# Linear attention and a gated layer on one core: the queues of all engines through the attention written out in steps

## The chip, the cores and the metric

The kernel runs on one core of a Trainium2 chip. The metric is device time in microseconds (us). The core has a matrix engine (TensorE, PE in the profile), a vector engine (VectorE, DVE), a scalar engine (ScalarE, ACT), GpSimd (POOL) and an engine that issues transfers (SyncE, SP). Each works through a queue of its own, and semaphores hold an instruction until what it needs is there.

## What is computed

First comes linear attention over 8 batches of 8 heads, 576 positions and 64 dimensions, with 128 features. Its output, 4608 rows of 512, then goes through a gated layer with 1536 hidden units.

```python
def phi(x):
    proj = np.einsum('bhsd,df->bhsf', x, w_phi)
    proj = proj - np.max(np.abs(proj), axis=-1, keepdims=True)
    return np.concatenate([np.exp(proj), np.exp(-proj)], axis=-1)
q_p, k_p = (phi(q), phi(k))
kv = np.einsum('bhsf,bhsd->bhfd', k_p, v)
z = np.sum(k_p, axis=2)
num = np.einsum('bhsf,bhfd->bhsd', q_p, kv)
den = np.einsum('bhsf,bhf->bhs', q_p, z)[..., None] + 1e-06
...
gate = 1.0 / (1.0 + np.exp(-(x @ w_gate)))
val = x @ w_val
return (gate * val @ w_out).astype(np.float32)
```

## The kernel before

**The steps of the attention.** Two heads are worked together, so there are 32 steps, four to a batch. A step i has these pieces:

- `q_half` (twice) and `k_heads`, `k_rest`: projections pq and pk on TensorE. ScalarE copies pq into d; VectorE takes the maximum mx of each row of pk, subtracts it (dk), and ScalarE takes the exponentials ek. For the first two steps (`DIRECT`) ScalarE reads pk itself.
- `q_max`: VectorE finds the maximum over the features of the queries (pm, pn), spreads it (mb) and subtracts it from d.
- `kv`: the products of keys and values (kvz), copied by ScalarE (kvt). `turn` transposes it (tp, then the copy kv).
- `q_exp`: ScalarE's exponentials eq of the queries, read from d.
- `num`: numerators nm and denominators dp, copied by ScalarE into ex and dr.
- `norm` and `scale`: the denominators go through three transfers, dn (out of dr), den (to memory, after VectorE's reciprocal) and rb (back, spread over the rows). VectorE then multiplies ex by rb (xp), and xp is stored to `xscr`.

From step 4 on GpSimd adds up ek (su) so that kvz needs fewer matmuls.

**The gated layer.** The 1536 hidden units are 12 groups of 128. The first five (`JA`) are worked in chunks of 256 rows between the pieces of the attention; the other seven follow in a second phase (`rest_chunks`), in chunks of 512 rows. Each product of a row and a weight is three matmuls of high and low parts (xh, xl, wh, wl). An item of the first phase is either a `half` (12 matmuls into gv, for the gate's or the value's 128 units) or a `half_out` (15 matmuls into acc, copied by ScalarE into y and stored). After the second half of a pair, `gated` makes the gated hidden units: t and u on ScalarE, three operations on VectorE, hh on ScalarE, hl on VectorE. The weights arrive as 64-bit floats and are split by `from_f64`, five VectorE operations and one ScalarE operation a tile; `TILES` says how many tiles are asked for by which step. gv has two buffers, acc one, and five PSUM banks rotate through all the attention's products.

**What sets the order.** TensorE's order is the program's. `fill` is called four times a step and puts in as many items as are due; items of a batch become due `LAG` calls after the batch's last step is queued. All other engines and the transfers are ordered by the tool's scheduler. It is steered by `attend`, which gives the attention a higher priority, and by `issue_after`, which ties weights behind the last subtraction of the queries (`marks`).

Of the kernel before, what the change touches and what calls it, by code (L numbers as in the profile page):

```python
# [37 lines left out]
PRIORITY = 400  # L38
RATE = 3.0
LAG = (5, 8)  # L40
TILES = (1, 2, 4, 7, 11, 15)
# [3 lines left out]
def attention_moe(  # L45
# [29 lines left out]
    def from_f64(h, l, raw, mid, sp, nb, name):  # L75
# [10 lines left out]
        if mid is None:  # L86
            rest, unit = hi, lo
            vec.tensor_scalar(
                hi, hi, 16, 0x01FF0000, op0=ALU.logical_shift_left, op1=ALU.bitwise_and
            )  # L90
            vec.scalar_tensor_tensor(
                hi, lo, 16, hi, op0=ALU.logical_shift_right, op1=ALU.bitwise_or
            )
        else:
            words = mid.rearrange("p (n two) -> p n two", two=2)
            rest, unit = words[:, :, 0], words[:, :, 1]
            vec.tensor_scalar(rest, rest, 0x01FFFFFF, None, op0=ALU.bitwise_and)
# [5 lines left out]
    def load_weights(j, m, wp, sp, nb, twice):  # L103
# [7 lines left out]
        load, mid = nc.sync.dma_start(raw, w_moe[j, :, m, :].bitcast(U32)), None  # L111
        if twice:

            mid = sp.tile([P, 2 * DM], U32, tag="wmid", name=f"wmid{j}_{m}", bufs=nb)
            nc.sync.dma_start(
                mid[:, : 2 * DM - 1].bitcast(U16),
                w_moe[j, :, m, :].bitcast(U16)[:, 1 : 4 * DM - 1],
            )
        return load, *from_f64(wh[:, ms], wl[:, ms], raw, mid, sp, nb, f"{j}_{m}")
# [41 lines left out]

    def half_units(js, mp, ps_gv, ps_acc):
        xs, hs, gvs, cs = {}, {}, {}, set()

        def begin(c, marks=()):
            if c in cs and c not in xs:
                xh, xl, raw = x_tiles(mp, CH, f"1_{c}")
                nc.sync.dma_start(raw, xscr[c])
                with ExitStack() as stack:
                    behind(stack, marks)  # L170
                    split(xh, xl, raw)
                xs[c] = xh, xl

        def half(c, i, m):
            begin(c)
# [5 lines left out]
            if m == 1:  # L181
                hs[c, i] = gated(gv[:, 0, :], gv[:, 1, :], CH, mp, 6, n)
                if i >= 1:
                    begin(c + 1, hs[c, i][2])

        def half_out(c, t):
            acc = ps_acc.tile([P, DM], F32, tag="acc", name=f"acc1_{c}_{t}")
            for i, j in enumerate(js):
                mm_out(acc, t, hs[c, i], j, i == 0, i == len(js) - 1)
            y = mp.tile([P, DM], F32, tag="y", name=f"y1_{c}_{t}", bufs=1)  # L190
# [3 lines left out]
        def chunk(c):  # L194
# [74 lines left out]
    with ExitStack() as actx:  # L269
        wp1 = actx.enter_context(tc.tile_pool(name="wp1", bufs=1))  # L270
# [19 lines left out]
        with tc.high_priority(offset=2 * PRIORITY):  # L290
            nc.sync.dma_start(wk, w_phi)
# [4 lines left out]
        loaded, ks, ds, kvs, marks, rbs = {}, {}, {}, {}, [], {}  # L296
# [10 lines left out]
        def load_kv(i):  # L307
            b, p = steps[i]
            n = f"{b}_{p}"
            kx = at.tile([P, 5 * P], F32, tag="kin", name="k" + n)  # L310
            nc.sync.dma_start(kx, k[b, p])
            vx = at.tile([P, 10, D], F32, tag="vin", name="v" + n)
            nc.sync.dma_start(vx, v[b, p])
            loaded["k", i], loaded["v", i] = kx, vx

        def q_half(i, hf):
# [11 lines left out]
            for hd in range(2):  # L328
                act.copy(d[:, hd, cs], pps[hd])

        def k_exp(i, g, pp, ns):
            n = f"{i}_{g}"
            mx = at.tile([P, 4], F32, tag="mx", name="mx" + n)
            vec.tensor_reduce(  # L334
                mx[:, :ns], pp[:, :ns, :], axis=AX.X, op=ALU.max,
                apply_absolute_value=True,
            )
            e = at.tile([P, ns, 2 * F], F32, tag=f"ek{ns}", name="ek" + n, bufs=6 - ns // 2)
            if i < DIRECT:
                mn = at.tile([P, 4], F32, tag="mn", name="mn" + n)  # L340
                vec.tensor_scalar(mn[:, :ns], mx[:, :ns], -1.0, None, op0=ALU.mult)
                for t in range(ns):
                    for sg in (1, 0):
                        act.activation(
                            e[:, t, sg * F : sg * F + F], pp[:, t, :], AF.Exp,
                            bias=(mn, mx)[sg][:, t : t + 1], scale=1.0 - 2.0 * sg,
                        )
            else:
                dk = at.tile([P, ns, F], F32, tag=f"dk{ns}", name="dk" + n)
                vec.tensor_tensor(  # L350
                    dk, pp[:, :ns, :],
                    mx[:, :ns].unsqueeze(2).broadcast_to([P, ns, F]),
                    op=ALU.subtract,
                )
                for sg in range(2):
                    act.activation(  # L356
                        e[:, :, sg * F : sg * F + F], dk, AF.Exp, scale=1.0 - 2.0 * sg
                    )
            ks.setdefault(i, []).append(e)

        def k_heads(i):
# [8 lines left out]
            for hd in range(2):  # L370
                k_exp(i, hd, pps[hd], 4)

        def k_rest(i):
            kx = loaded.pop(("k", i))
            pp = bank([P, 4, F], f"pk{i}_2")
            nc.tensor.matmul(pp[:, 0, :], kx[:, 4 * P :], wk, start=True, stop=True)
            k_exp(i, 2, pp, 1)
            if i < EARLY:
                return

# [12 lines left out]

        def q_max(i):
            d = ds[i]
# [8 lines left out]
            )  # L404
            vec.tensor_copy(pn[0:64], pm[64:128])
# [5 lines left out]
            vec.tensor_tensor(pm, pm, pn, op=ALU.max)  # L411
            vec.transpose(  # L412
# [3 lines left out]
            marks.append(vec.tensor_tensor(d, d, mb, op=ALU.subtract))  # L416

        def kv(i):
# [26 lines left out]
            kvt = at.tile([P, 3 * F], F32, tag="kvt", name=f"kvt{i}")  # L445
# [11 lines left out]
        def q_exp(i):  # L457
            d = ds.pop(i)
            es = []
            for sg in range(2):  # L460
                e = at.tile([P, 2, S], F32, tag=f"eq{sg}", name=f"eq{i}_{sg}")
                act.activation(e, d, AF.Exp, scale=1.0 - 2.0 * sg)
                es.append(e)
            ds[i] = es

        def num(i):
            es, w = ds.pop(i), kvs.pop(i)
# [22 lines left out]
            act.copy(dr, dp)  # L490
            for hf in range(2):
                act.copy(ex[:, hf * HS : hf * HS + HS], nms[hf])
            rbs[i] = (ex, dr)

        def norm(i):
            ex, dr = rbs[i]
            dn = at.tile([P, 9], F32, tag="dn", name=f"dn{i}")
            rb = at.tile([P, S], F32, tag="rb", name=f"rb{i}", bufs=1)
            nc.sync.dma_start(
                dn, dr.rearrange("(o r) c -> o r c", r=Q)[:, 0, :]  # L500
            )
            vec.tensor_scalar(dn, dn, 1e-6, None, op0=ALU.add)
            vec.reciprocal(dn, dn)
            nc.sync.dma_start(dens[i].rearrange("h (r c) -> (h r) c", c=9), dn)
            for hd in range(2):
# [3 lines left out]
            rbs[i] = (ex, rb)  # L509

        def scale(i):
            b, p = steps[i]
            ex, rb = rbs.pop(i)
            xp = at.tile([P, S], F32, tag="xp", name=f"xp{i}")
            vec.tensor_tensor(xp, ex, rb, op=ALU.mult)
            t = 0
            for c in range(S // CH if b == 0 else 0):
# [4 lines left out]
                split(xs[c][0][:, ps], xs[c][1][:, ps], xp[:, c * CH : c * CH + CH])  # L522
            while t < S:
# [9 lines left out]
        cdone = wdone = spot = last = 0  # L533
        due = 0.0

        def fill():
# [7 lines left out]
            due += min(RATE, sum(c for c, _ in ready) / max(1, left))  # L544
            while ready and due >= ready[0][0] / 2:
                cost, f = ready.pop(0)
                f()
                due -= cost

# [6 lines left out]
        def attend(f, *a):  # L556
            with tc.high_priority(offset=PRIORITY):
                f(*a)

        def finish(i):  # L560
            attend(norm, i)
            attend(scale, i)
            if i % NP == NP - 1:
                queue(i // NP)

        N = len(steps)
        for i in range(-1, N + 1):
            if i == -1:
                attend(load_q, 0)
                attend(load_kv, 0)  # L570
            if i + 2 < N:
                attend(load_q, i + 2)
                attend(load_kv, i + 2)
            if i + 1 < N:
                attend(q_half, i + 1, 0)
                attend(k_heads, i + 1)
                fill()
                attend(q_half, i + 1, 1)
                attend(k_rest, i + 1)
                attend(q_max, i + 1)  # L580
                fill()
            if i >= EARLY + 1:
                attend(q_exp, i - 1)
            if 0 <= i < N:
                attend(kv, i)
            if i >= EARLY + 1:
                attend(num, i - 1)
# [92 lines left out]
```

## Time and profile before

| | |
|---|---|
| three runs | 1416.51, 1418.56 (median), 1420.45 us |
| the profiled execution | 1415.93 us |
| its span, first to last instruction | 1414.1 us |
| TensorE busy | 1257.5 us (89%), 9096 matmuls |
| TensorE loading weights | 1000.8 us (71%) |
| VectorE busy | 799.1 us (57%) |
| ScalarE busy | 530.0 us (37%) |
| GpSimd busy | 173.0 us (12%) |
| mean granted TensorE clock | 0.943 |
| moved by DMA | 133.42 MB, 94 GB/s |

Busy time is a mean over parts that differ: the profile is best read by stretches. A row of the view by stretches ("windows") has start and end, length, the busy time of each engine with its number of instructions, the granted clock of TensorE (1.00 is full speed), the share of time that the DMA engines were busy, and GB/s. In the view of waits a row reads: who waited, for whom, us in total, times, the longest. In a timeline a row has start, length, engine, line, operation, what it writes and reads, and in brackets the idle time just before it and what ended it. L138 and L145 are the lines of the matmuls of the gated layer.

### The profile page before, as it was taken

Reading aid. Unit: us, or ns where it says so; the run is one execution under the profiler, and the core shown is the slowest. Engines: PE = TensorE matmul, PEld = TensorE weight load, DVE = VectorE, ACT = ScalarE, POOL = GpSimd, SP = SyncE. Lnnn points to the kernel's source line nnn. Section 1 sums busy time; section 2 is a strip of 40 time slices with the busy share of each in tenths; the row PEclk is TensorE's granted clock in tenths of the full one; section 3 lists DMA queues with packets and bytes.
Section 4 is the critical chain, followed back from the end, with each engine's and each line's share of the span. In section 5 each row is a group of like instructions: output and inputs, shape, how many; then the busy total and the mean of one; then the engine's idle time right before and its main releaser. Section 6 shows DMA issues by size and latency. Waiting matters only on the chain.

```text
span 1414.1 us, 22819 instructions
## 1 busy us (share of the span) xinstructions
PE 1257.5 (89%) x9096; PEld 1000.8 (71%) x9096; DVE 799.1 (57%) x1527; ACT 530.0 (37%) x1133; POOL 173.0 (12%) x230
## 2 busy tenths in 40 slices
PE   6674878967987988889899799999999999999998
PEld 3453656656775776767677789788888888888887
DVE  4798757655766666575563863773434434244333
ACT  5554444544444544544443433332212212122121
POOL 0042123221312213231130000000000000000000
PEclk8996788988998999989999999999999999999999
DMA  5376613322222232322213630541202112012010
GB/s 182 127 234 203 206 60 118 104 74 77 87 88 78 87 102 77 104 72 77 77 57 97 210 133 24 186 142 60 90 3 88 53 37 90 30 60 87 3 60 30
DMA packets 81737, 133.42 MB, mean 94 GB/s; under 512 B 18656, under 2 KB 38240, under 8 KB 81632
## 3 DMA queue, kind: packets, MB, share of 16 engines
q1 hardware_dynamic: 81632, 131.98, 28.4%
q8 instruction: 71, 1.16, 0.3%
q14 instruction: 34, 0.28, 0.1%
HBM read 93.91 MB, written 28.46 MB: 87 GB/s over the span
## 4 chain that ended last, share of the span: by engine, by line
PE 57%; DVE 20%; DMA 13%; ACT 5%; issue 4%; SPq 1%; DVEq 0%; ACTq 0%
PE acc L145 18%; PE g L138 12%; PE v L138 12%; PE gv L138 7%; DMA rb<-den 4%; DMA dn<-dr 3%; DMA den<-dn 3%; DVE mx L334 2%; PE kvz L426 2%; PE nm L475 2%; DVE pn L410 2%; DVE mb L412 2%; DVE pm L401 1%; DVE dk L350 1%; ACT ek L356 1%
## 5 line engine op out<-in xcount | busy, mean ns | idle before, releaser
L138 PE MATMUL gv<-xh,wh 128*128 128x256 f32 x720 | 220.6, 306 | 65.2 <-DVE t L158 26.1
L145 PE MATMUL acc<-wh,hh 128*128 128x512 f32 x432 | 180.0, 417 | 38.4 <-ACT y L191 38.4
L138 PE MATMUL gv<-xl,wh 128*128 128x256 f32 x720 | 212.0, 294 | 1.4 <-DVE xl L63 1.4
L138 PE MATMUL gv<-xh,wl 128*128 128x256 f32 x720 | 211.7, 294 | 0.1
L138 PEld LDWEIGHTS gv<-xh,wh 128*128 128x128 f32 x720 | 145.5, 202 | 81.4 <-issue 27.5
L62 ACT CAST hh<-u 128x256 fp32r<-128x256 f32 (+1 forms) x153 | 75.7, 495 | 339.0 <-DVE u L159 339.0
L145 PE MATMUL acc<-wl,hh 128*128 128x512 f32 x432 | 175.4, 406 | 0.0
L145 PE MATMUL acc<-wh,hl 128*128 128x512 f32 x432 | 174.4, 404 | 0.3 <-DVE hl L63 0.3
L157 DVE TENSOR_SCALAR t<-t 128x256 uint32<-128x256 uint32 (+1 forms) x153 | 58.4, 382 | 203.2 <-ACT t L154 203.0
L138 PEld LDWEIGHTS gv<-xl,wh 128*128 128x128 f32 x720 | 146.1, 203 | 2.1 <-DVE xl L63 1.9
L138 PEld LDWEIGHTS gv<-xh,wl 128*128 128x128 f32 x720 | 146.0, 203 | 0.7 <-DVE wl L99 0.6
L145 PEld LDWEIGHTS acc<-wh,hh 128*128 128x128 f32 x432 | 85.2, 197 | 63.9 <-ACT y L191 42.4
L63 DVE TENSOR_TENSOR hl<-u,hh 128x256 fp32r<-128x256 f32 (+1 forms) x153 | 83.9, 548 | 57.5 <-ACT hh L62 56.9
L356 ACT ACTIVATE ek<-dk 128x512 f32<-128x512 f32 x180 | 82.3, 520 | 76.9 <-DVE dk L350 76.9
L384 POOL TENSOR_TENSOR su<-ek 128x256 f32<-128x256 f32 x56 | 43.8, 782 | 540.7 <-issue 295.4
L145 PEld LDWEIGHTS acc<-wh,hl 128*128 128x128 f32 x432 | 85.1, 197 | 20.6 <-DVE hl L63 1.0
L138 PE MATMUL g<-xh,wh 128*128 128x512 f32 x252 | 99.0, 393 | 0.0
L138 PE MATMUL v<-xh,wh 128*128 128x512 f32 x252 | 98.6, 391 | 0.0
L138 PE MATMUL g<-xh,wl 128*128 128x512 f32 x252 | 98.5, 391 | 0.0
L138 PE MATMUL g<-xl,wh 128*128 128x512 f32 x252 | 98.5, 391 | 0.0
L138 PE MATMUL v<-xl,wh 128*128 128x512 f32 x252 | 98.3, 390 | 0.0
L138 PE MATMUL v<-xh,wl 128*128 128x512 f32 x252 | 98.1, 389 | 0.0
(85 smaller groups left out, 2165.6 us busy)
## 6 DMA issues: line engine op xcount, KB each, us to landing
wraw<-w_moe SPq DMA_DIRECT2D x36, 512.0 KB
xl<-xs SPq DMA_DIRECT2D x34, 512.0 KB
k<-k SPq DMA_DIRECT2D x32, 320.0 KB
v<-v SPq DMA_DIRECT2D x32, 320.0 KB
q<-q SPq DMA_DIRECT2D x32, 288.0 KB
wh<-wtop SPq DMA_DIRECT2D x36, 256.0 KB
rb<-den SPq DMA_DIRECT2D x64, 144.0 KB
ys<-y SPq DMA_DIRECT2D x36, 256.0 KB
```

The costliest lines, as they stand in the source:

```text
L62: a = act.copy(h, x)
L63: return a, vec.tensor_tensor(l, x, h.bitcast(F32), op=ALU.subtract)
L138: nc.tensor.matmul(o, a[:, ws], x[:, cs], start=i == 0, stop=i == 11)
L145: nc.tensor.matmul(acc, a[:, ts], w[:, ws], start=first and i == 0, stop=last and i == 2)
L157: vec.tensor_scalar(tu, tu, 0x7FFFFFFF, None, op0=ALU.bitwise_and)
L334: vec.tensor_reduce(mx[:, :ns], pp[:, :ns, :], axis=AX.X, op=ALU.max, apply_absolute_value=True,)
L356: act.activation(e[:, :, sg * F : sg * F + F], dk, AF.Exp, scale=1.0 - 2.0 * sg)
L384: pool.tensor_tensor(su[:, hd, :], es[hd][:, 0, :], es[hd][:, 1, :], op=ALU.add)
L410: vec.tensor_copy(pn[a * 32 : a * 32 + 32], pm[o * 32 : o * 32 + 32])
L412: vec.transpose(mb.rearrange("p h s -> p (h s)"), pm.unsqueeze(2).broadcast_to([P, nj, 32]),)
L426: nc.tensor.matmul(kvz[o : o + Q, : 2 * F], vx[:, 2 * t + hd, o % D : o % D + Q], (e0, e1)[hd][:, t, :] if t < 4 else e2[:, 0, :], start=t ...
L475: nc.tensor.matmul(nms[hf][o : o + Q, :], w[:, sg, o : o + Q], es[sg][:, o // D, cs], start=sg == 0, stop=sg == 1, tile_position=(0, o),)
```

## The change

The scheduler no longer orders anything in the attention: `manual_schedule` is entered for all engines, so each engine and each DMA queue runs in the order in which the program names its instructions. Work that must wait for another engine is written as a generator that stops at `yield`. `start` runs it to its first stop, and `tick` runs each started one to its next stop. A tick follows each item, and `fill` makes at least three of them. So the maximum, the subtraction and the exponentials of the keys, the gate, the loads of x, the normalization and the weights each come a given number of ticks apart.

The places of the pieces move too. `num` and the normalization of step i now always run in step i + 1 (before, the first four steps did it in their own), `q_exp` follows `turn`, and the keys come ahead of the queries. The two acc items of a chunk no longer follow each other; y gets two buffers; eq, kvt and one size of dk lose one of two; hh and hl get seven. Raw weights, their shifted copy and wtop have two buffers, with loads two tiles ahead. `LAG` becomes (7, 9), `TILES` (1, 3, 5, 8, 11, 15).

VectorE's queue around the normalization of step 14, before (dn, xp and the gate's t, u, hl; the number after a name is step or chunk):

```order
L416 TENSOR_TENSOR d16_3706<-d16_3706,mb16_3782 128x1152
L502 TENSOR_SCALAR dn14_3882<-dn14_3882 128x9
L503 RECIPROCAL dn14_3882<-dn14_3882 128x9
L515 TENSOR_TENSOR xp14_3890<-ex14_3825,rb14_3883 128x576
L157 TENSOR_SCALAR t1_4_1_3921<-t1_4_1_3921 128x256
L158 SCALAR_TENSOR_TENSOR t1_4_1_3921<-t1_4_1_3921,gv1_4_1_3895 128x256
```

The same place of VectorE's queue in the change:

```order
L602 TENSOR_SCALAR dn14_3886<-dn14_3886 128x9
L603 RECIPROCAL dn14_3886<-dn14_3886 128x9
L414 TENSOR_REDUCE mx17_0_3970<-pk17_0_3960 128x4
L414 TENSOR_REDUCE mx17_1_3973<-pk17_1_3961 128x4
L221 TENSOR_SCALAR t1_4_2_3945<-t1_4_2_3945 128x256
L222 SCALAR_TENSOR_TENSOR t1_4_2_3945<-t1_4_2_3945,gv1_4_2_3931 128x256
L223 SCALAR_TENSOR_TENSOR u1_4_2_3944<-u1_4_2_3944,t1_4_2_3945 128x256
L438 TENSOR_TENSOR dk17_0_3999<-pk17_0_3960,mx17_0_3970 128x512
L438 TENSOR_TENSOR dk17_1_4001<-pk17_1_3961,mx17_1_3973 128x512
L226 TENSOR_TENSOR hl1_4_2_3947<-u1_4_2_3944,hh1_4_2_3946 128x256
L613 TENSOR_TENSOR xp14_4023<-ex14_3854,rb14_3887 128x576
```

Between the reciprocal and xp lies the way of the denominators to memory and back. Nothing stood there before; now there are eight instructions of step 17 and of the gate.

ScalarE's queue behind the copy dr of step 14, before (eq are the exponentials of the queries, y1_3_1 the copy of an acc item, kv the copy of the turned product):

```order
L490 COPY dr14_3853<-dp14_3828 128x288
L462 ACTIVATE eq16_0_4331<-d16_3706 128x1152
L462 ACTIVATE eq16_1_4333<-d16_3706 128x1152
L191 ACTIVATE y1_3_1_3873<-acc1_3_1_3857 128x512
L455 COPY kv15_3880<-tp15_3876 128x384
```

And in the change:

```order
L592 COPY dr14_3882<-dp14_3857 128x288
L256 ACTIVATE y1_3_1_3905<-acc1_3_1_3889 128x512
L209 CAST xh1_5_3812<-xl1_5_3813 128x1024
L553 COPY kv15_3927<-tp15_3923 128x384
L244 ACTIVATE t1_4_2_3945<-gv1_4_2_3931 128x256
L245 ACTIVATE u1_4_2_3944<-gv1_4_2_3931 128x256
L561 ACTIVATE eq15_0_3952<-d15_3451 128x1152
L561 ACTIVATE eq15_1_3954<-d15_3451 128x1152
```

The exponentials moved from ahead of y to behind kv, and they are those of step 15, whose d was finished a step earlier, instead of step 16.

The diff, cut to its core:

```diff
-PRIORITY = 400
-LAG = (5, 8)
-TILES = (1, 2, 4, 7, 11, 15)
+LAG = (7, 9)
+TILES = (1, 3, 5, 8, 11, 15)
+TICKS = 3
...
+    def weight_tile(w, raw, mid, wp, sp):
...
+        vec.tensor_scalar(top, hi, 0x7FFFFE00, None, op0=ALU.bitwise_and)
+        act.activation(top, top, AF.Relu, bias=ebias, scale=8.0)
+        vec.tensor_scalar(rest, rest, 0x01FFFFFF, None, op0=ALU.bitwise_and)
+        yield
...
+        nc.sync.dma_start(h.bitcast(U32), top)
+        yield
...
+    tasks = []
+    def start(g):
+        if next(g, tasks) is not tasks:
+            tasks.append(g)
+    def tick():
+        for g in list(tasks):
+            if next(g, tasks) is tasks:
+                tasks.remove(g)
...
+        def load_x(c):
+            xh, xl, raw = x_tiles(mp, CH, f"1_{c}")
+            xs[c] = xh, xl
+            nc.sync.dma_start(raw, xscr[c])
+            for _ in range(3):
+                yield
+            act.copy(xh, raw)
+            yield
+            vec.tensor_tensor(xl, raw, xh.bitcast(F32), op=ALU.subtract)
...
+        def gate(c, i, n):
...
+            vec.scalar_tensor_tensor(u, u, 1.0, t, op0=ALU.min, op1=ALU.mult)
+            act.copy(hh, u)
+            yield
+            vec.tensor_tensor(hl, u, hh.bitcast(F32), op=ALU.subtract)
...
+            if m == 0:
...
+                act.activation(t, gv[:, 0, :], AF.Tanh, scale=0.5)
+                act.activation(u, gv[:, 0, :], AF.Exp)
+            else:
+                start(gate(c, i, n))
...
-                if i == 0 and c:
-                    items += outs(c - 1)
+                if i < 2 and c:
+                    items += outs(c - 1)[i : i + 1]
...
+        actx.enter_context(tc.manual_schedule())
...
+        def norm(i, ex, dr):
...
             nc.sync.dma_start(dn, dr.rearrange("(o r) c -> o r c", r=Q)[:, 0, :])
+            for _ in range(3):
+                yield
             vec.tensor_scalar(dn, dn, 1e-6, None, op0=ALU.add)
             vec.reciprocal(dn, dn)
             nc.sync.dma_start(dens[i].rearrange("h (r c) -> (h r) c", c=9), dn)
+            yield
             for hd in range(2):
...
+            for _ in range(4):
+                yield
             xp = at.tile([P, S], F32, tag="xp", name=f"xp{i}")
             vec.tensor_tensor(xp, ex, rb, op=ALU.mult)
...
             while ready and due >= ready[0][0] / 2:
                 cost, f = ready.pop(0)
                 f()
+                tick()
                 due -= cost
+                n += 1
+            for _ in range(TICKS - n):
+                tick()
...
+        start(weigh())
         for i in range(-1, N + 1):
...
             if i + 1 < N:
+                keys(i + 1)
+                copies(q_half(i + 1, 0))
                 fill()
+                copies(q_half(i + 1, 1))
+                rest(i + 1)
+                start(q_max(i + 1))
                 fill()
             if 0 <= i < N:
+                kv(i)
+            if i >= 1:
+                num(i - 1)
+                if (i - 1) % NP == NP - 1:
+                    queue((i - 1) // NP)
             fill()
             if 0 <= i < N:
+                turn(i)
+                start(q_exp(i))
+                if i + 2 < N:
+                    load_v(i + 2)
             fill()
```

More of the change, by code (lines that the diff above doesn't have):

```diff
@@ L85, in from_f64 @@
         nc.sync.dma_start(h.bitcast(U32), top)
[L86 to L97, printed above, removed]
+        rest, unit = hi, lo
+        vec.tensor_scalar(
+            hi, hi, 16, 0x01FF0000, op0=ALU.logical_shift_left, op1=ALU.bitwise_and
+        )
+        vec.scalar_tensor_tensor(
+            hi, lo, 16, hi, op0=ALU.logical_shift_right, op1=ALU.bitwise_or
+        )
         vec.tensor_scalar(unit, top, 0xFF800000, None, op0=ALU.bitwise_and)
@@ L327, in q_half @@
                 )
[L328 to L359, printed above, removed]
+            return [(d[:, hd, cs], pps[hd]) for hd in range(2)]
         def k_heads(i):
@@ L369, in k_heads, with k_exp, k_sum @@
                     )
[L370 to L378, printed above, removed]
-                return
+            return pps
+        def k_exp(i, gs, pps, ns):
+            mxs, es = [], []
+            for g, pp in zip(gs, pps):
+                n = f"{i}_{g}"
+                mx = at.tile([P, 4], F32, tag=f"mx{g}", name="mx" + n)
+                vec.tensor_reduce(
+                    mx[:, :ns], pp[:, :ns, :], axis=AX.X, op=ALU.max,
+                    apply_absolute_value=True,
+                )
+                mxs.append(mx)
+                es.append(
+                    at.tile([P, ns, 2 * F], F32, tag=f"ek{g}", name="ek" + n)
+                )
+            ks.setdefault(i, []).extend(es)
+            yield
+            if i < DIRECT:
+                for g, pp, mx, e in zip(gs, pps, mxs, es):
+                    mn = at.tile([P, 4], F32, tag=f"mn{g}", name=f"mn{i}_{g}")
+                    vec.tensor_scalar(mn[:, :ns], mx[:, :ns], -1.0, None, op0=ALU.mult)
+                    for t in range(ns):
+                        for sg in (1, 0):
+                            act.activation(
+                                e[:, t, sg * F : sg * F + F], pp[:, t, :], AF.Exp,
+                                bias=(mn, mx)[sg][:, t : t + 1], scale=1.0 - 2.0 * sg,
+                            )
+                return
+            dks = []
+            for g, pp, mx in zip(gs, pps, mxs):
+                dk = at.tile([P, ns, F], F32, tag=f"dk{g}", name=f"dk{i}_{g}", bufs=1)
+                vec.tensor_tensor(
+                    dk, pp[:, :ns, :],
+                    mx[:, :ns].unsqueeze(2).broadcast_to([P, ns, F]),
+                    op=ALU.subtract,
+                )
+                dks.append(dk)
+            yield
+            for dk, e in zip(dks, es):
+                for sg in range(2):
+                    act.activation(
+                        e[:, :, sg * F : sg * F + F], dk, AF.Exp, scale=1.0 - 2.0 * sg
+                    )
+                yield
+        def k_sum(i):
             es = ks[i]
@@ L392, in k_rest, with copies, keys, rest @@
             es.append(su)
+        def copies(cs):
+            for o, x in cs:
+                act.copy(o, x)
+        def keys(i):
+            pps = k_heads(i)
+            start(k_exp(i, (0, 1), pps, 4))
+        def rest(i):
+            kx = loaded.pop(("k", i))
+            pp = bank([P, 4, F], f"pk{i}_2")
+            nc.tensor.matmul(pp[:, 0, :], kx[:, 4 * P :], wk, start=True, stop=True)
+            def go():
+                yield from k_exp(i, (2,), [pp], 1)
+                if i >= EARLY:
+                    yield
+                    k_sum(i)
+            start(go())
         def q_max(i):
+            yield
             d = ds[i]
@@ L444, in kv @@
                     )
-            kvt = at.tile([P, 3 * F], F32, tag="kvt", name=f"kvt{i}")
+            kvt = at.tile([P, 3 * F], F32, tag="kvt", name=f"kvt{i}", bufs=1)
             act.copy(kvt, kvz)
@@ L457, in q_exp @@
         def q_exp(i):
+            yield
             d = ds.pop(i)
@@ L508, in norm @@
                 )
[L509 to L513, printed above, removed]
+            for _ in range(4):
+                yield
             xp = at.tile([P, S], F32, tag="xp", name=f"xp{i}")
             vec.tensor_tensor(xp, ex, rb, op=ALU.mult)
-            t = 0
             for c in range(S // CH if b == 0 else 0):
@@ L533, in attention_moe, with weigh @@
         cdone = wdone = spot = last = 0
+        wq = []
+        def weigh():
+            raws = [raw_tile(w, at) for w in range(2)]
+            for w in range(3 * JA):
+                while not wq:
+                    yield
+                wq.pop(0)
+                yield from weight_tile(w, *raws.pop(0), wp1, at)
+                if w + 2 < 3 * JA:
+                    raws.append(raw_tile(w + 2, at))
+                yield
         due = 0.0
@@ L574, in attention_moe @@
+        load_k(0)
+        load_q(0)
+        load_v(0)
+        load_k(1)
+        load_q(1)
+        load_v(1)
+        start(weigh())
+        for i in range(-1, N + 1):
+            if 0 <= i and i + 2 < N:
+                load_q(i + 2)
+                load_k(i + 2)
+            while i >= 0 and wdone < TILES[min(i, len(TILES) - 1)]:
+                wq.append(wdone)
+                wdone += 1
             if i + 1 < N:
-                attend(q_half, i + 1, 0)
-                attend(k_heads, i + 1)
+                keys(i + 1)
+                copies(q_half(i + 1, 0))
@@ L588, in attention_moe @@
             fill()
             if 0 <= i < N:
-                attend(turn, i)
-            if i >= EARLY + 1:
-                finish(i - 1)
+                turn(i)
+                start(q_exp(i))
+                if i + 2 < N:
+                    load_v(i + 2)
             fill()
-            if 0 <= i < EARLY:
-                attend(q_exp, i)
-                attend(num, i)
-                finish(i)
-            while i >= 0 and wdone < TILES[min(i, len(TILES) - 1)]:
-                with tc.issue_after(marks[-1].ins):
-                    load_weights(wdone // 3, wdone % 3, wp1, at1, 1, True)
-                wdone += 1
@@ L606, in attention_moe @@
             f()
+            tick()
+        while tasks:
+            tick()
     with ExitStack() as bctx:
```

139 lines of the change are left out of this document (75 added, 64 removed).

## The prediction

> **What bounds the kernel now.** I read the trace in this order: busy time by stage, TensorE's waits by stage, the stretches where TensorE runs without a gap, then one step in which it stops. PE is TensorE, DVE VectorE, ACT ScalarE, SP the engine that issues the DMAs. The columns of the first view are start and end, length, busy time of PE, its weight loads, DVE, ACT and GpSimd, then granted clock and DMA share.
>
> ```profile
> 0.00:96.40 96.40, 64.36 (x752) 37.73 (x752) 66.06 (x143) 54.51 (x131) 12.92 (x20) 0.88 0.52 176
> 96.40:145.50 49.10, 28.39 (x228) 22.35 (x227) 42.16 (x82) 20.80 (x44) 14.78 (x16) 0.74 0.65 214
> 145.50:744.50 599.00, 514.77 (x4932) 398.91 (x4935) 385.96 (x755) 274.96 (x633) 145.32 (x194) 0.92 0.28 89
> 744.50:891.50 147.00, 131.17 (x924) 116.49 (x917) 82.41 (x193) 50.96 (x120) 0.00 (x0) 0.95 0.35 115
> 891.50:1414.10 522.60, 518.85 (x2268) 425.34 (x2267) 222.47 (x358) 128.78 (x208) 0.00 (x0) 1.00 0.21 68
> ```
>
> The borders are the first item of the gated layer (96.4), kvz of step 6 (145.5), kvz of step 31 (to within 2 us) and the first g of the second phase (891.5). The second phase has PE busy 99% at clock 1.00, and its code stays: 522.6 us are kept. All that can move is the 891.5 us ahead of it. There PE is the busiest engine, yet idle for 84.2 us between 145.5 and 744.5, and slowed. How long the same work takes without gaps is read from differences of start times:
>
> ```profile
> 452.46 0.50 PE L145 MATMUL acc<-wh,hh 128*128 128x512 f32 x1
> 456.10 0.76 PE L325 MATMUL pq<-q,wk 64*128 64x288 f32 x4
> ...
> 473.53 0.76 PE L325 MATMUL pq<-q,wk 64*128 64x288 f32 x4
> 475.10 0.38 PE L138 MATMUL gv<-xh,wh 128*128 128x256 f32 x1
> 478.16 0.76 PE L325 MATMUL pq<-q,wk 64*128 64x288 f32 x4
> 479.09 0.36 PE L138 MATMUL gv<-xh,wh 128*128 128x256 f32 x1
> 482.13 2.37 PE L426 MATMUL kvz<-ek,v 128*32 128x256 f32 x40
> 484.53 2.12 PE L475 MATMUL nm<-eq,kv 128*32 128x288 f32 x32
> 487.56 0.39 PE L138 MATMUL gv<-xh,wh 128*128 128x256 f32 x1
> 490.54 0.49 PE L453 MATMUL tp<-ident,kvt 128*128 128x128 f32 x3
> 490.78 0.48 PE L145 MATMUL acc<-wh,hh 128*128 128x512 f32 x1
> ```
>
> One attention step costs PE 1.57 (473.53 to 475.10) + 0.93 (478.16 to 479.09) + 5.43 (482.13 to 487.56) + 0.24 (the turn) = **8.17 us**. Two gv halves cost 3.06, 3.04 or 2.98, so 1.51 each; an acc item 3.64. From kvz 6 to kvz 31 PE has 25 steps, and in the order of before 120 halves and 24 acc: 204 + 181 + 87 = 473 us. It took 599. The 126 us of loss are 84 of idle and 42 of slower running. The idle time, in the view of waits (us in total, times, longest), first for this stage, then for 744.5 to 891.5:
>
> ```profile
> PE acc L145 <- ACT y L191: 30.7, 8, 7.5
> PE gv L138 <- DVE t L158: 18.2, 8, 4.3
> PE gv L138 <- ACT xh L62: 14.5, 2, 7.9
> ...
> PE gv L138 <- DVE t L158: 7.9, 3, 5.8
> PE acc L145 <- ACT y L191: 7.7, 6, 3.1
> ```
>
> Neither ACT (275 of 599) nor DVE (386 of 599) is full. They are late because each runs its queue in order and something ahead in it waits. One such step, DVE, ACT and DMA issues (SPq) together:
>
> ```profile
> 413.01 1.17 ACT L462 ACTIVATE eq<-d 128x1152 f32<-128x1152 f32 x1 [1.97 <-DVE d L416]
> 414.08 0.38 ACT L490 COPY dr<-dp 128x288 f32<-128x288 f32 x1
> 414.49 0.59 SPq L499 DMA_DIRECT2D dn<-dr  x1
> 416.50 0.17 DVE L502 TENSOR_SCALAR dn<-dn 128x9 f32<-128x9 f32 x1 [3.60 <-DMA dn<-dr]
> 416.95 0.32 SPq L504 DMA_DIRECT2D den<-dn  x1
> 418.40 1.10 SPq L506 DMA_DIRECT2D rb<-den  x2
> 421.96 0.76 DVE L515 TENSOR_TENSOR xp<-ex,rb 128x576 f32<-128x576 f32 x1 [2.84 <-DMA rb<-den]
> 423.54 0.40 ACT L62 CAST hh<-u 128x256 fp32r<-128x256 f32 x1 [3.76 <-DVE u L159]
> ...
> DVE xp L515 <- DMA rb<-den: 64.9, 23, 5.5
> DVE dn L502 <- DMA dn<-dr: 51.6, 19, 7.0
> ```
>
> The exponentials eq of the queries stand in ACT's queue ahead of dr and y, though nobody needs them yet, and wait for DVE. dr is late by that, its transfer starts late, DVE stands 3.60 us at dn, and 2.84 us more at xp, with the gate (t, u) behind it. Over the stage DVE stands 116.5 us at those two places: 4.7 us a step.
>
> **The change part by part.** No arithmetic is removed. PE has the same matmuls; between kvz 6 and kvz 31 they are now 126 halves and 24 acc, between kvz 31 and the second phase 51 halves and 12 acc (52 and 12 before).
>
> *First stage, to kvz 6.* num now follows one step late from the start, the first item comes one step later, and all 15 weight tiles are worked by step 5. The windows of before for DVE's operations on wtop alone (three of the five that a tile needs), and DVE's first work:
>
> ```profile
> 0.00:145.50 145.50, 20.36 (x35) 0.83 0.56 189
> ...
> 7.32 1.29 DVE L334 TENSOR_REDUCE mx<-pk 128x4 f32<-128x512 f32 x2 [6.03 <-PE pk L366]
> ```
>
> 35 operations of 0.58 us are between eleven and twelve tiles by 145.5. Five such operations are an estimated 2.9 us a tile, so the four tiles more are 12 us. DVE was busy 66.1 + 42.2 = 108.2 us. With the four tiles and three gates fewer (four operations each; at about the 0.40 of the hh row an estimated 1.7 us), it has 115 us of work up to kvz 6. To that I add the 7 us before its first work and five norms that DVE reaches early, at 2.84 us each: 136 us. Below lies 122 (no such wait), above 157 (the 145.5 of before and the 12). I take **136**, since two tiles in flight cover more of the weights than one did.
>
> *Middle stage.* The floor is 204 + 126 x 1.51 + 24 x 3.64 = 482 us. What of the 84 us of waits stays? The y wait goes: two gv halves or an attention group now stand between the acc items, eq stands behind y, and y has two buffers. The xh wait goes: the load is issued three ticks ahead of its cast. The waits at dn and xp leave DVE's path: eight instructions stand between recip and xp, where there were none. I keep the wait for t of the gate (18.2), since gv still has two buffers and the gate's operations are only spread differently, and the same share of the slower running, 42 x 18.2 / 84 = 9. The stage is **509 us**, 20.4 a step. Bounds: 482 with nothing left, 545 with half of the loss kept. DVE has 386 / 25 = 15.4 us of work in a step and 0.2 for the three more gates; that fits if its waits stay under 4.8.
>
> *Last stage.* PE alone runs without gaps here (the chain of waits, pieces with their length):
>
> ```profile
> 827.76 14.40 PE gv L138 x120
> 842.16 3.43 PE acc L145 x15
> ...
> 846.27 3.69 PE acc L145 x15
> ```
>
> That gives 1.44 us a half, 3.43 or 3.69 an acc. 51 x 1.44 + 12 x 3.56 + 8.7 for the last attention groups is 125 us; before it was 126 of 147. The waits for y (7.7) go, since the acc items no longer follow each other (842.16 + 3.43 to 846.27 is 0.68 us each chunk). The wait for t (7.9) stays, since DVE still has the next phase's weights in the same queue, with 2 us of clock: **135**, bounds 125 and 147.
>
> *Sum.* 136 + 509 + 135 = 780; with 522.6 the span is 1302.6. Around the span lie 1415.93 - 1414.10 = 1.83 us: **1304 us**. The profiled execution is 2.6 us under the median 1418.56, within its spread.
>
> *The clock.* After long idle PE runs slowly:
>
> ```profile
> 443.84 0.58 PE L138 MATMUL gv<-xh,wh 128*128 128x256 f32 x1 [6.61 <-ACT xh L62]
> ...
> 450.88 0.76 PE L325 MATMUL pq<-q,wk 64*128 64x288 f32 x4
> ```
>
> Two halves and a turn took 7.04 us instead of 3.2. The 42 us of slower running thus hang on idle time, which is why I let them shrink with it. The Trainium skill, TensorE: Matmul & The Clock Gate, "HAM oscillation — how this bites in real kernels", says that idle gaps over about 3.4 us put the clock back to half; the row agrees on the half, while the recovery here took about 7 us. By that page all 42 us would go and the sum would be 9 us lower.
>
> **The rivals.**
>
> *A, DVE becomes the bound.* If dn and xp stay exposed (4.7 a step) and DVE keeps waiting for ACT at the gate,
>
> ```profile
> DVE t L157 <- ACT t L154: 39.1, 21, 2.9
> ```
>
> 1.6 a step, a step is 15.6 + 4.7 + 1.6 = 21.9 us, the stage 547, the time **1342**. For it: steps with three gates have little slack. Against it: the eight instructions before xp are work that DVE has anyway.
>
> *B, slower.* A fixed order places dn and xp in DVE's queue whatever the transfers do. If ACT's casts, the banks and so PE come to wait there, the chain from dn's issue to xp (414.49 to 421.96, 7.47 us) lies bare in each of 25 steps: 187 us more, **1491**. It decides once a step loses more than 4.5 us beyond my 20.4 (620.5 us for the stage would be the time of before). Against it: before, with nothing between dn and xp, PE lost 84 us in all, 3.4 a step. The Trainium skill's same page, Part 1, calls the queues of ScalarE and VectorE strictly first in, first out; the step at 413 agrees.
>
> *C, the clock stays low on short gaps.* The middle stage keeps its 42 us: **1337**. Against it:
>
> ```profile
> 550.00:600.00 50.00, 45.79 (x454) 36.73 (x454) 33.73 (x68) 24.11 (x57) 12.31 (x17) 1.00 0.31 97
> ```
>
> 4.2 us of idle in small pieces, clock 1.00. The Trainium skill's same page, "A second HAM failure mode: psum-queue depth-cycling", says that frequent micro-idling alone can make the clock oscillate; this row speaks against it.
>
> *D, nothing gained.* The new waits repay what the old ones cost, about **1416**.
>
> **How the numbers follow.** Forecast 0.64, A 0.18, B 0.08, C 0.06, D 0.04. About 0.3% is what a measurement here can tell from no change. Forecast, A and C are faster (0.88), D the same (0.04), B slower (0.08). Bounds: 122 + 482 + 125 gives 1253, 157 + 545 + 147 gives 1373. These hold A and C too, so the range is 1255 to 1375.
>
> **What would show it.** Right: kvz 6 near 136 us, kvz 31 near 645, the second phase from about 780; y gone from PE's waits, dn and xp under 1 us a step on DVE, granted clock above 0.96 in the middle. Wrong: DVE over 85% busy there (A), PE waiting for nm, kvz or tp behind ACT (B), clock under 0.93 with few waits (C), or a second phase that starts late behind its weights.

## The result: 0.8% faster, a tenth of what was forecast

The changed kernel takes 1407.3 us (median of four, 1405.7 to 1410.2), the kernel before 1418.4: a ratio of 0.9924, 95% interval 0.9902 to 0.9945. The forecast was 1304, its range 1255 to 1375. The sign was right; of the 115 us expected, 11 came.

The view by stretches of the changed kernel, cut at the same events as before (kvz 6, kvz 31, the first g of the second phase):

```profile
0.00:151.30 151.30, 93.78 (x922) 56.54 (x922) 112.04 (x231) 72.41 (x168) 23.62 (x34) 0.79 0.63 205
151.30:719.00 567.70, 505.81 (x4968) 385.92 (x4968) 373.43 (x755) 281.11 (x639) 151.65 (x197) 0.97 0.29 88
719.00:881.20 162.20, 135.20 (x948) 116.69 (x947) 80.30 (x186) 56.37 (x121) 0.00 (x0) 0.98 0.32 106
881.20:1403.80 522.60, 518.38 (x2266) 425.14 (x2265) 222.17 (x357) 128.51 (x208) 0.00 (x0) 1.00 0.20 67
```

| stage | before | forecast | after |
|---|---|---|---|
| to kvz 6 | 145.5 | 136 | 151.3 |
| kvz 6 to kvz 31 | 599.0 | 509 | 567.7 |
| to the second phase | 147.0 | 135 | 162.2 |
| second phase | 522.6 | 522.6 | 522.6 |

The middle gained a third of what it should, and the last stage, which holds hardly anything but items of the gated layer, became 15 us longer. TensorE's waits after the change, whole span:

```profile
PE gv L164 <- ACT u L245: 66.9, 65, 2.4
...
PE gv L164 <- ACT xh L209: 17.1, 3, 5.8
PE pq L393 <- ACT kv L553: 12.4, 3, 5.9
PE nm L575 <- ACT d L469: 12.2, 4, 4.9
...
PE pq L393 <- ACT d L469: 10.6, 6, 4.9
```

The first row is new: before, TensorE never waited there for u. Of it, 42.3 us (40 times) lie in the middle stage and 24.6 us (25 times) in the last. kv, d and nm belong to the first stage. y has all but gone (one wait of 0.7 us). One of the 65 waits, in the timeline of the changed kernel:

```profile
715.17 0.28 PE L164 MATMUL gv<-xh,wl 128*128 128x256 f32 x1
715.49 0.38 ACT L244 ACTIVATE t<-gv 128x256 f32<-128x256 f32 x1 [1.20 <-PE gv L164]
715.76 0.38 ACT L245 ACTIVATE u<-gv 128x256 f32<-128x256 f32 x1
715.90 0.29 DVE L221 TENSOR_SCALAR t<-t 128x256 uint32<-128x256 uint32 x1 [0.80 <-ACT t L244]
716.20 0.39 PE L164 MATMUL gv<-xh,wh 128*128 128x256 f32 x1 [0.75 <-ACT u L245]
```

The first row is the last matmul of a pair's first half; the fifth is the first of its second half. Between them ScalarE reads the first half twice. The second half writes other columns, but of the same tile gv, and the program puts a semaphore there: TensorE stands until u is through. There are 90 pairs. Where an attention group stands between the halves the wait is hidden; in the last stage hardly any does, and 25 of some 26 pairs wait.

### The profile page after: what moved, and what is told of

Same layout as the page of the kernel before. It is cut to its first block, busy times and chain, and to the rows that moved or that the text cites. A ratio compares the mean times of both kernels' runs of the same rounds, so it can differ in the third digit from the quotient of the medians.

```text
span 1403.8 us, 22704 instructions
## 1 busy us (share of the span) xinstructions
PE 1253.2 (89%) x9096; PEld 984.3 (70%) x9096; DVE 787.9 (56%) x1527; ACT 538.4 (38%) x1133; POOL 175.3 (12%) x230
## 4 chain that ended last, share of the span: by engine, by line
PE 73%; DVE 10%; ACT 9%; DMA 5%; issue 2%; SPq 1%; DVEq 0%; ACTq 0%
PE acc L171 21%; PE gv L164 15%; PE g L164 12%; PE v L164 12%; PE kvz L524 4%; PE nm L575 3%; ACT ek L447 2%; PE dp L584 2%; ACT t L244 2%; DMA rb<-den 1%; PE pk L403 1%; ACT u L245 1%; ACT eq L561 1%; PE pq L393 1%; DMA den<-dn 1%
## 5 line engine op out<-in xcount | busy, mean ns | idle before, releaser
L164 PEld LDWEIGHTS gv<-xh,wh 128*128 128x128 f32 x720 | 141.9, 197 | 115.5 <-ACT u L245 84.2
L164 PE MATMUL gv<-xh,wl 128*128 128x256 f32 x720 | 208.2, 289 | 0.0
L171 PE MATMUL acc<-wh,hh 128*128 128x512 f32 x432 | 172.9, 400 | 0.7 <-ACT y L256 0.7
L171 PE MATMUL acc<-wl,hh 128*128 128x512 f32 x432 | 170.0, 393 | 0.0
L171 PE MATMUL acc<-wh,hl 128*128 128x512 f32 x432 | 169.1, 391 | 0.0
L62 ACT CAST hh<-u 128x512 fp32r<-128x512 f32 x63 | 39.1, 621 | 201.1 <-DVE u L185 201.1
L224 ACT CAST hh<-u 128x256 fp32r<-128x256 f32 x90 | 36.5, 406 | 197.8 <-DVE u L223 197.6
L183 DVE TENSOR_SCALAR t<-t 128x512 uint32<-128x512 uint32 x63 | 26.8, 426 | 138.6 <-ACT t L180 138.4
L524 PE MATMUL kvz<-ek,v 128*32 128x256 f32 x1280 | 87.7, 426 | 15.9 <-issue 8.7
L180 ACT ACTIVATE t<-g 128x512 f32<-128x512 f32 x63 | 37.6, 597 | 150.8 <-PE g L164 150.7
```

Source lines behind the costliest of these rows:

```text
L62: a = act.copy(h, x)
L164: nc.tensor.matmul(o, a[:, ws], x[:, cs], start=i == 0, stop=i == 11)
L171: nc.tensor.matmul(acc, a[:, ts], w[:, ws], start=first and i == 0, stop=last and i == 2)
L180: act.activation(t, g, AF.Tanh, scale=0.5)
L183: vec.tensor_scalar(tu, tu, 0x7FFFFFFF, None, op0=ALU.bitwise_and)
L224: act.copy(hh, u)
```

## The experiments

| run | us | ratio to before, 95% interval |
|---|---|---|
| after | 1407.3 | 0.9924 (0.9902 to 0.9945) |
| e1_gate_late | 1331.3 | 0.9393 (0.9366 to 0.9419) |
| e2_two_tiles | 1331.3 | 0.9390 (0.9365 to 0.9416) |
| e3_before_gate_early | 1463.5 | 1.0321 (1.0293 to 1.0349) |
| e4_gate_late_x_ahead | 1306.9 | 0.9219 (0.9192 to 0.9245) |
| f1_xp_later_at_first | 1289.3 | 0.9083 (0.9067 to 0.9099) |
| f2_relu_later | 1306.3 | 0.9202 (0.9185 to 0.9220) |
| f3_both | 1290.2 | 0.9092 (0.9069 to 0.9114) |
| g1_norm_at_once | 1505.0 | 1.0601 (1.0579 to 1.0623) |
| h1_y_as_before | 1317.6 | 0.9283 (0.9265 to 0.9301) |
| h3_eq_ahead | 1312.2 | 0.9241 (0.9219 to 0.9264) |
| h4_y_and_eq | 1335.7 | 0.9405 (0.9388 to 0.9422) |
| k1_two_tiles_best | 1293.0 | 0.9111 (0.9097 to 0.9124) |

The kernel before was timed beside each group of four: medians 1417.3 (e), 1419.1 (f, g) and 1418.8 (h, k).

### The gate's t and u between the halves

One part of the change undone:

```diff
             if m == 0:
...
-                act.activation(t, gv[:, 0, :], AF.Tanh, scale=0.5)
-                act.activation(u, gv[:, 0, :], AF.Exp)
             else:
+                u, t = hs[c, i][:2]
+                act.activation(t, gv[:, 0, :], AF.Tanh, scale=0.5)
+                act.activation(u, gv[:, 0, :], AF.Exp)
                 start(gate(c, i, n))
```

> The change with one part undone: t and u are issued after the pair's second half, as before, so no semaphore stands between the halves. Main theory (the 66.9 us at 'gv waits for u' were put there by the change, 90 pairs of about 0.75 us): this wait is gone, the last stage falls from 162 to about 147 us, the middle from 568 to 520 to 540, the waits for t of before (26 us in all) come back in part; 1340 to 1370 us. Rival (VectorE or the transfers are late anyway and TensorE waits elsewhere as long): 1395 to 1415 us, with the lost wait found again under t, hl or kv.

The halves in tiles of their own, t and u left between them:

```diff
-                gvs[c, i] = ps_gv.tile([P, 2, CH], F32, tag="gv", name="gv" + n)
+                gvs[c, i] = [
+                    ps_gv.tile([P, CH], F32, tag=f"gv{x}", name=f"gv{x}" + n, bufs=1)
+                    for x in range(2)
+                ]
```

> The change, but the gate's and the value's half have tiles (and so PSUM banks) of their own, one buffer each; t and u stay between the halves. Main theory: the second half no longer waits for u. The second half of the next pair now has to wait until VectorE's t of this pair has read the value's tile: at most 90 waits, 1.5 us of slack each. 1340 to 1380 us. Rival (TensorE waits elsewhere as long): 1395 to 1415 us.

And the suspected cost put alone into the kernel before:

```diff
             mm_in(gv[:, m, :], xs[c], js[i], m, CH)
+            if m == 0:
...
+                act.activation(t, gv[:, 0, :], AF.Tanh, scale=0.5)
+                act.activation(u, gv[:, 0, :], AF.Exp)
+                gates[c, i] = u, t
...
-                hs[c, i] = gated(gv[:, 0, :], gv[:, 1, :], CH, mp, 6, n)
+                hs[c, i] = gated(gv[:, 0, :], gv[:, 1, :], CH, mp, 6, n, gates.pop((c, i)))
```

> The kernel before, with nothing changed but t and u of the first phase issued between the halves. Main theory: the same wait for u appears there, 90 pairs of 0.75 us or a bit more = 67 us or more, less up to 26 us for the waits at t that shrink: 1455 to 1490 us. Rival (such a wait only moves other idle time of TensorE): 1415 to 1430 us.

The first two come out at the same 1331.3 us, 76 under the change and 9 under the least that I had expected of either; the third comes out 46 over before, as expected. The middle and last stretch of e1_gate_late, then TensorE's longest waits there in its middle:

```profile
149.00:667.10 518.10, 495.07 (x4974) 385.19 (x4974) 375.77 (x757) 278.61 (x638) 154.65 (x197) 0.97 0.32 96
667.10:802.90 135.80, 127.29 (x941) 113.19 (x941) 80.07 (x186) 55.16 (x120) 0.00 (x0) 0.99 0.38 124
```

```profile
PE gv L164 <- ACT xh L209: 18.5, 3, 6.7
PE gv L164 <- DVE xl L211: 2.2, 3, 0.9
```

Against the change the middle got 49.6 us shorter, where 42.3 us of waits were recorded, and the last stage 26.4, where 24.6 were. So the wait is a net loss. That e2 wins the same with t and u where the change put them shows that it is the shared tile, not the early reading, that costs. The Trainium skill, PSUM — Partial Sum Buffer, "PSUM bank collisions raise a hardware error", says that a matmul's write and another engine's read must not meet in one bank and the same partitions, whichever columns they touch, and tells one to guard by bank and quadrant and not by address. e2 fits this: once the halves no longer share a tile, 2.0 us (3 times) are left of the wait for u. Whether the wait goes by the tile or by the bank no run tells, and none shows what a collision does. I had expected 1340 or more because the waits for VectorE's t of before (26 us) might return; they hardly did (4.0 us in e1, 7.1 in e2, over the whole span).

In the kernel before with the early reading, the wait is larger than what it costs:

```profile
PE gv L138 <- ACT u L189: 100.6, 68, 6.1
```

100.6 us of waits made the kernel 46 us slower: part of it took the place of waits that were there already. The waits for t (26.1 us before) are gone, those for y fell from 38.4 to 15.6 us, those for xh from 14.5 to 5.5.

### The load of x at the start of a batch

Three waits for xh are left in e1's middle stage. This is SP's part of one of them in the changed kernel, then ScalarE's and VectorE's:

```profile
328.47 0.40 ACT L592 COPY dr<-dp 128x288 f32<-128x288 f32 x1 [0.57 <-PE dp L584]
328.90 0.59 SPq L599 DMA_DIRECT2D dn<-dr  x1
329.54 0.47 SPq L206 DMA_DIRECT2D xl<-xs  x1
...
332.93 1.04 ACT L209 CAST xh<-xl 128x1024 fp32r<-128x1024 f32 x1 [4.06 <-DMA xl<-xs]
334.01 1.23 DVE L211 TENSOR_TENSOR xl<-xl,xh 128x1024 fp32r<-128x1024 f32 x1 [2.68 <-ACT xh L209]
```

The first chunk of a batch isn't known yet when the chunk ahead of it runs, so `half` starts its load itself, runs four ticks at once and needs the data; in SP's queue the load stands behind dn, which waits for dr. The edit, on top of e1:

```diff
+        def ahead(c):
+            cs.add(c)
+            begin(c)
...
+            if coming and coming[0][0] - 2 <= spot:
+                ahead(coming[0][1][0])
             while coming and coming[0][0] <= spot:
```

> As e1, and the x of the first chunk of a batch is loaded two calls of fill earlier instead of in the item that needs it. Theory: the three waits for xh (17.1 us, with the slow stretches of 3 to 6 us behind each) go: 17 to 30 us under e1. Rival (the load stands behind dn in the queue of the transfers and is as late as before): the same as e1 within 5 us.

24.4 us less. In the middle stage of e4_gate_late_x_ahead TensorE is idle for only 6.6 us, and its clock is full:

```profile
151.60:647.30 495.70, 489.14 (x4974) 378.78 (x4973) 371.58 (x757) 278.07 (x639) 158.20 (x196) 1.00 0.34 101
```

### The first stage

It is still 151.6 us long there. Its waits on ScalarE and VectorE in e4_gate_late_x_ahead:

```profile
ACT wtop L134 <- DVE wtop L133: 33.2, 10, 6.1
...
ACT xh L62 <- DVE xp L618: 25.7, 4, 8.2
...
DVE xp L618 <- DMA rb<-den: 17.0, 4, 6.0
```

And one normalization of the first batch in its timeline, from the reciprocal to TensorE:

```profile
89.27 0.21 DVE L608 RECIPROCAL dn<-dn 128x9 f32<-128x9 f32 x1
...
89.65 0.42 SPq L609 DMA_DIRECT2D den<-dn  x1
...
95.01 1.13 SPq L612 DMA_DIRECT2D rb<-den  x2
...
98.70 0.76 DVE L618 TENSOR_TENSOR xp<-ex,rb 128x576 f32<-128x576 f32 x1 [5.61 <-DMA rb<-den]
...
99.49 0.71 ACT L62 CAST xh<-xp 128x256 fp32r<-128x256 f32 x2 [7.78 <-DVE xp L618]
...
102.20 0.67 ACT L474 COPY d<-pq 128x288 f32<-128x288 f32 x2
...
102.63 2.15 PE L580 MATMUL nm<-eq,kv 128*32 128x288 f32 x16 [5.35 <-ACT d L474]
```

Four queues stand in a row: rb waits 5.4 us for den, VectorE for rb, ScalarE for xp, TensorE for the copy d behind ScalarE's casts. ScalarE also stands for VectorE at wtop. Two edits take one each:

```diff
-            for _ in range(4):
+            for _ in range(8 if b == 0 else 4):
                 yield
...
             vec.tensor_tensor(xp, ex, rb, op=ALU.mult)
+            if b == 0:
+                yield
```

> As e4, and in the first batch xp comes four ticks later and the casts into xh one tick after xp. Theory one (until kvz 6 the way of the denominators through the loaded DMA engines lies bare: VectorE stands 17.0 us at xp, ScalarE 25.7 us at xh behind it, and TensorE waits for d and kv behind that): 12 to 25 us under e4, kvz 6 at about 130 to 140 us. Theory two (VectorE's 111 us of work and the order of its queue set the first stage): within 5 us of e4, the waits only change their names.

```diff
-        act.activation(top, top, AF.Relu, bias=ebias, scale=8.0)
         vec.tensor_scalar(rest, rest, 0x01FFFFFF, None, op0=ALU.bitwise_and)
         yield
+        act.activation(top, top, AF.Relu, bias=ebias, scale=8.0)
+        yield
```

> As e4, and ScalarE's part of a weight tile (wtop) is issued one tick after VectorE's, so that ScalarE need not stand there (33.2 us in the first stage). Theory one (any wait in ScalarE's queue is handed on to TensorE): 8 to 20 us under e4. Theory two (VectorE sets the first stage, ScalarE waits there with nothing else to do): within 5 us of e4, or later, as a weight tile takes a tick more.

> f1 and f2 together, over e4. Theory one: the gains of both, 20 to 40 us under e4, kvz 6 at 115 to 132 us. Theory two: within 5 us of e4.

The first gives 17.6 us by the medians (e4 was timed in another group; against f2, timed beside it, it is 17.0), the second nothing that can be told from noise, both together what the first gives. The first stretch of f1_xp_later_at_first and of f2_relu_later:

```profile
0.00:134.10 134.10, 89.65 (x918) 55.85 (x918) 110.59 (x230) 73.90 (x167) 25.37 (x35) 0.82 0.69 232
```

```profile
0.00:148.50 148.50, 91.38 (x919) 56.19 (x919) 109.51 (x224) 73.10 (x167) 23.61 (x34) 0.78 0.60 205
```

In f1 VectorE's wait at xp is all but gone, and ScalarE's wait at xh with it; ScalarE's longest wait, at wtop, is as long as ever:

```profile
DVE xp L618 <- DMA rb<-den: 0.5, 1, 0.5
```

```profile
ACT wtop L134 <- DVE wtop L133: 34.9, 13, 5.6
```

Moving wtop a tick later didn't take it away either:

```profile
ACT wtop L136 <- DVE wtop L133: 32.8, 14, 6.5
```

So f2 doesn't show what this wait is worth, as it is still there. What the two runs show is that the stage got 17.5 us shorter with ScalarE's longest wait unchanged: the shorter one, at the end of a chain that VectorE stood in too, was the one that cost. f1 moves xp and the casts together; which of the two did it was not tried. With f1, VectorE is busy 110.6 of 134.1 us, the fullest engine there; that it now sets the stage is likely but not shown.

### What the ticks of the normalization are worth

```diff
             nc.sync.dma_start(dn, dr.rearrange("(o r) c -> o r c", r=Q)[:, 0, :])
-            for _ in range(3):
-                yield
             vec.tensor_scalar(dn, dn, 1e-6, None, op0=ALU.add)
             vec.reciprocal(dn, dn)
             nc.sync.dma_start(dens[i].rearrange("h (r c) -> (h r) c", c=9), dn)
-            yield
...
-            for _ in range(4):
-                yield
             xp = at.tile([P, S], F32, tag="xp", name=f"xp{i}")
...
+            yield
```

> As e4 with the ticks of the normalization taken out: dn, the reciprocal, den, rb, xp and the store are issued in one piece, with nothing of VectorE's between them. Theory (the ticks are what took the waits at dn and xp off VectorE's path): VectorE stands about 7.5 us in each of 31 steps, 16 more us of its work in a step make 24 to 25 us a step against 19.8 in e4: 110 to 190 us over e4. Rival (VectorE had room for it, as it has 372 us of work in 496): under 40 us over e4.

1505.0, 198 over e4 and somewhat more than expected. In the middle stage of g1_norm_at_once, which takes 648.4 us:

```profile
DVE xp L613 <- DMA rb<-den: 131.2, 24, 6.7
...
DVE dn L605 <- DMA dn<-dr: 29.6, 17, 4.4
```

VectorE stands 160.8 us there, and the stage is 152.7 us longer than in e4, 6.1 a step; the first and the last stage grow by 20 and 24 us. In the change itself the same two rows of the middle stage are 13.7 and 9.0 us, 0.9 us a step.

### What took the wait for y away

The prediction gave three reasons in one breath: the acc items are apart, y has two buffers, and eq stands behind y. Undone in two parts, on top of f1:

```diff
-            y = mp.tile([P, DM], F32, tag="y", name=f"y1_{c}_{t}")
+            y = mp.tile([P, DM], F32, tag="y", name=f"y1_{c}_{t}", bufs=1)
...
-                if i < 2 and c:
-                    items += outs(c - 1)[i : i + 1]
+                if i == 0 and c:
+                    items += outs(c - 1)
```

> As f1, with the acc items of a chunk next to each other again and one buffer for y. Theory one (the places of the acc items are what took TensorE's wait for y, 30.7 and 7.7 us before, away): 25 to 45 us over f1. Theory two (y was late because the exponentials eq stood ahead of it, and they no longer do): only the time of one y and its semaphores stays, 18 chunks of about 0.7 to 1.3 us, 8 to 20 us over f1.

```diff
             vec.tensor_tensor(d, d, mb, op=ALU.subtract)
+            yield from q_exp(i)
...
-                start(q_exp(i))
```

> As f1, with the exponentials eq issued right behind the subtraction of d, ahead of xh, kv and y, as the scheduler had them before (eq has two buffers again, xp one to make room). Theory one (the places of the acc items took the wait for y away): within 8 us of f1. Theory two (eq's place did): ScalarE stands about 2 us for d and works 2.2 at eq ahead of kv or y in each of 25 steps, and TensorE loses 10 to 40 us of it.

> h1 and h3 together (hh and hl with six buffers, as before). The wait for y of the kernel before should come back whole by either theory, 30 to 60 us over f1; if h1 and h3 are near f1 each, only their meeting makes it, and this one alone is late.

The first costs 28.3 us, the second 22.9, both together 46.4: they add up, nearly. But only the first brings back a wait for y, and only part of it. TensorE's wait for y over the whole span in h1_y_as_before and in h4_y_and_eq:

```profile
PE acc L171 <- ACT y L261: 10.5, 8, 4.0
```

```profile
PE acc L171 <- ACT y L261: 17.2, 9, 4.1
```

Before it was 38.4 us. I had expected it whole in h4; less than half came. In h1 17.5 of the 28.3 us are in the last stage (151.4 against 133.9), with 8.9 us of the wait for y, 5.8 for t and a clock of 0.94 against 0.97. In h3_eq_ahead, TensorE's wait for y is 2.0 us. There, ScalarE stands for VectorE at eq again (62.3 us in the middle stage, for d and, behind it in VectorE's queue, dn). The middle stage of f1_xp_later_at_first and of h3_eq_ahead:

```profile
134.10:629.40 495.30, 490.11 (x4996) 379.22 (x4999) 373.52 (x758) 279.36 (x642) 158.53 (x196) 0.99 0.34 101
```

```profile
136.00:651.60 515.60, 497.08 (x4972) 383.38 (x4971) 368.33 (x755) 273.38 (x637) 157.95 (x198) 0.99 0.33 97
```

20.3 of the 22.9 us are lost here, and TensorE's longest waits in it are for the copies d, not for kv or y:

```profile
PE pq L398 <- ACT d L474: 6.5, 7, 1.6
PE nm L580 <- ACT d L474: 5.8, 2, 4.5
```

So theory two holds in that eq ahead costs TensorE time, but what TensorE then waits for is neither kv nor y. h3 also gives xp a single buffer; in h4 xp keeps two (pn gets one instead), and eq ahead costs 18.1 us there over h1, so most of it is eq's place. One buffer for y and the places of the acc items were undone together, so neither has a price of its own.

### The fastest version

> The edits of f1 with e2's two one-buffer tiles in place of t and u behind the pair. TensorE's waits in f1 are under 15 us behind the first stage, so no more can be won: within 6 us of f1.

1293.0: no gain over f1. f1_xp_later_at_first at 1289.3 us is the fastest kernel here (f3_both, 1290.2, can't be told from it), 9.2% under before (ratio 0.9083, 0.9067 to 0.9099) and 8.4% under the change.

## Why the prediction was right in its sign and wrong in its size

**The step that failed** is this: "I keep the wait for t of the gate (18.2), since gv still has two buffers and the gate's operations are only spread differently". They are spread across the write of the second half into the same tile. The rows of before had no wait at that place, so nothing was booked; I asked who waits for t's data and not who waits for t's reading. It costs 76 us by e1 and e2, in the middle and in the last stage. The last stage, forecast at 135, is 135.8 once it is gone. By e1 the rest of the change wins some 86 us, and this wait took 76 of them back: the sign of the forecast came out right by a narrow margin.

**The xh wait** ("goes: the load is issued three ticks ahead of its cast") stayed for the first chunk of a batch, where the ticks run out at once. It costs 24 us by e4; 20.7 of it are waits in e1 (18.5 and 2.2 in the rows above), and once they are gone the clock of the middle stage is 1.00 instead of 0.97. Reading `half` would have shown it.

**The first stage** was forecast at 136 and took 151.3. VectorE's longest waits there in the changed kernel:

```profile
DVE xp L613 <- DMA rb<-den: 18.3, 5, 5.2
DVE mx L414 <- PE pk L403: 5.1, 1, 5.1
DVE pm L496 <- ACT d L469: 4.9, 2, 2.4
DVE dn L602 <- DMA dn<-dr: 2.3, 2, 1.2
```

What the sum counted came as counted: 112.0 us of work (115 forecast, with the 3.3 tiles still missing rounded up to four), about 6 until the first maximum (7) and 18.3 at xp (14), 136 in all. The other 15 us of the 39.3 that VectorE is idle are small waits, for the copies d, for dn and the like, which the sum put at nothing. f1 removes the waits at xp, and with them ScalarE's for xp and most of TensorE's for d at nm: rival B's bare chain, in the first batch alone. The small waits stay in f1. So its 134.1 is near the forecast by luck: it is 12 us over the 122 of the bounds, which stood for a stage without waits at xp. No run tests the reason given for 136, that two tiles in flight cover more of the weights.

**The sum.** 1407.3 - 76.0 - 24.4 - 17.6 = 1289.3 us, which is f1; the edits stand on top of each other, so they add up by construction. The forecast of 1304 was the time of a kernel that has none of the first two and 14 us of the third. f1 is 15 us under it, nearly all in the middle stage (509 against 495.3): the 27 us that I kept for t and its clock didn't come (TensorE's 3.6 us of waits for t in f1 are in the last stage), while the floor of 482 was too low (TensorE is busy 490 us there).

**What held.** The second phase kept its 522.6. dn and xp left VectorE's path in the middle (0.9 us a step), and g1 gives that term its price: without the ticks the middle loses 152.7 us, 6.1 a step, where rival B had charged 7.47 a step, 187 us, for the bare chain. y went (0.7 us are left), but the reasons are shown only in part: undoing all three brings back 17.2 of 38.4 us. Rival A fell: VectorE has 373.5 of 495.3 us in f1's middle, 75%. Rival C fell: the clock of the middle rose from 0.92 to 0.97 with the change and to 1.00 in e4, when the long waits were gone. (The remark that all 42 us would go overlooks that one of the waits for t that the sum kept is 4.3 us long, over the 3.4 us that the prediction names.) Rival D, nothing gained, came nearest to the time, and by its own mechanism: a new wait repaid most of what the old ones had cost.

## What to carry to other kernels

When an instruction moves, list who waits for its *reads*, too: here a reader placed between two writes into one PSUM tile made the second writer wait, though they touch different columns, and a tile of its own for each part did as well as moving the reader back (1331.3 us both). In a hand-written order, check the start of each loop by itself; a distance in ticks that holds in the steady state may be empty for the first chunk and the first batch. And a long wait in the table of an engine is worth what stands behind it: f1 won 18 us by the chain that ended in 26 us at xh, and 35 us at wtop were still there.

## What the runs showed of the hardware beyond that

The clock bore many short gaps here. In the changed kernel's last stage TensorE stood 25 times for 24.6 us in all, about 1 us every 6.5 us, and its granted clock stayed at 0.98. The Trainium skill, TensorE: Matmul & The Clock Gate, "A second HAM failure mode: psum-queue depth-cycling", says that frequent micro-idling can make the clock oscillate; this row doesn't show it.

A small transfer took over twice as long where large ones had just been issued. In the first stage of e4, rb could be issued 5.4 and 5.5 us after den in two of the five steps (89.65 to 95.01 and 115.68 to 121.15), and in both three transfers of weights (256 to 512 KB each) had been issued in the 1.7 us before den. In the other three, with one of them or none there, it took 1.4 to 2.5 us. In the middle stage of the changed kernel it took 1.4 to 3.0, as here 2.2 us:

```profile
306.27 0.38 SPq L604 DMA_DIRECT2D den<-dn  x1
...
308.43 1.11 SPq L607 DMA_DIRECT2D rb<-den  x2
```

That the weights' transfers make den late fits these five steps; no run changes them alone.
